# Loading the K and V caches in pairs of tiles: a one-token attention kernel on one core

## The chip, the core and the metric

The kernel runs on one core of one Trainium2 chip. The metric is device time in microseconds (us), the median of several runs, lower is better. The kernel before takes 2529.17 us (three runs, 2528.84 to 2529.18). A profile is one further execution, recorded by the hardware profiler.

In what follows PE is TensorE (matmul), DVE is VectorE, ACT is ScalarE, SP is SyncE, which issues nearly all of the transfers. "L313" is line 313 of the kernel. A core has 16 DMA engines, which work off the transfers that were issued; a transfer spreads over all of them.

## What is computed

One token's attention over a long cache, beside a gated feed-forward, both mixed by a scalar gate. All data are bf16.

```
x: [1, 1, 512]   k_cache, v_cache: [1, 32 heads, 65536 positions, 128]
q = x @ wq                               # 32 heads of 128
scores = (q . k_cache) / sqrt(128)       # per head, 65536 of them
o = softmax(scores) @ v_cache            # per head, 128
a = concat(o) @ wo                       # [4096] @ [4096, 512]
b = (silu(x @ w_gate) * (x @ w_up)) @ w_down
g = sigmoid(sum(x * gate_w))
out = g * a + (1 - g) * b                # [1, 1, 512]
```

The two caches hold 537 MB each, and each number in them is used once. The weights (wq and wo 4 MB each, the feed-forward 5.5 MB) are small beside them.

## The kernel before

**Tiles.** A head's 65,536 positions are cut in four tiles (`G` = 4) of 128 x 128 positions: partition p of a tile holds 128 positions (`NB`) that stand one after the other in memory, each 128 numbers long. So a tile is 4 MB, a contiguous row of 32 KB in each of 128 partitions. There are 128 tiles of K and 128 of V, numbered n = 0 to 127 through all heads (`N`).

**Buffers.** K tiles, V tiles, wq, the feed-forward weights and the second half of wo share a ring of five buffers of 32 KB a partition (`SLOTS`). `take` hands out the buffer that has been free longest, `give` returns it. Nothing is scheduled by a planner: the kernel is written under a manual schedule, so that each engine, SP's queue of transfers included, runs its instructions in the order of the program text. A transfer into a buffer waits on SP until the instructions that read that buffer last are done, and all later transfers wait behind it.

**What happens to a K tile** (`products`, L236; `scores`, L254; `fold`, L268). DVE multiplies the tile by the head's q, which lies spread over all partitions in `q_bc` (L245), and adds the upper half of each 128 products to the lower half, once for the first four tiles, twice for the others (L249). PE sums what is left (64 or 32 columns) by matmuls with an identity matrix, four columns at a time, into a PSUM tile of 128 x 512 (L258: 16 or 8 matmuls). DVE folds the last four columns into the scores (L272).

**What happens when a head's four tiles are scored.** DVE takes the maximum of each partition (L278); ACT, PE and DVE make one maximum of all partitions (L280, L282, L287); ACT takes the exponentials and their sum (L291); PE sums over partitions (L299), and DVE makes the weight of the head (L304, L305). To start this early, the first K tile of the next head is multiplied in two halves of 64 positions, and the steps stand between them.

**What happens to a V tile** (`values`, L307). 32 matmuls of 512 columns (four positions each, L313) add exponentials times V into a PSUM tile of the head. When four tiles are done, `head_turn` (L329) brings the head's result to the partitions (L326, L342, L349), and `project` (L353) multiplies it by its rows of wo (L356) into two accumulators that stay in PSUM to the end. The last eight positions of the last tile are multiplied in another form (L334).

**The order.** wq and the first four K tiles are issued at once. `queries` (L145) makes q for all heads, by matmuls of 512 columns (L147) whose stationary operand is x spread over 128 columns, and ACT copies (L154). Then come the four K tiles of head 0, with the gate and the first half of the feed-forward between them (L176: 112 matmuls of one column). From tile 4 on, a list `steps` (L397) pairs a K tile n with a V tile v. In each step SP issues K tile n (already issued for n = 4) and V tile v, DVE and PE work on K tile n, and PE on V tile v. V starts four tiles behind K; from n = 40 on (`SPREAD`) a step in four carries no V tile until V stands eight tiles behind (`LAG`). The buffers allow some three transfers in flight beside the tiles in use. In the last eight steps only V tiles are left.

**wo.** Its first 16 heads' rows are loaded in four pieces of 512 KB into two small buffers of their own, one for every four heads; the other 16 heads' rows (`LATE`) are issued last of all, behind V, in four pieces, into a ring buffer. The last V tiles are issued in pieces too, ever smaller (`V_CUTS`), so that PE can begin on what has landed.

Of the kernel before, what the change touches and what calls it, by code (L numbers as in the profile page):

```python
# [11 lines left out]
P = 128  # L12
# [3 lines left out]
NB = 128  # L16
SLOTS = 5
# [5 lines left out]
LAG = 8  # L23
SPREAD = 40

WG = 4
LATE = 16
LATE_CUTS = (0, 5, 10, 14, LATE)
TURNED = 8
V_CUTS = {3: (0, 64, NB), 2: (0, 64, NB), 1: (0, 32, 64, 96, 112, NB - TURNED, NB)}  # L30
# [3 lines left out]
def kernel(  # L34
# [26 lines left out]
    QG = 4  # L61
    assert Dh == P and Sk % (NB * P) == 0 and NBH <= 512 and H % QG == 0 and G >= 2
# [5 lines left out]
    ppool = ctx.enter_context(tc.tile_pool(name="ppool", bufs=3))  # L68
    wo_pool = ctx.enter_context(tc.tile_pool(name="wo_pool", bufs=2))
# [11 lines left out]
    def take(name):  # L81
        slot = free.pop(0)
        held[name] = slot
        return ring.tile(
            [P, NB * Dh], bf16, name=name.split(".")[0], tag=f"slot{slot}"
        )
# [5 lines left out]
    consts.tile([P, 32], bf16, name="fill")  # L92
# [6 lines left out]
    QW = QG * Dh  # L99
    wq_t = take("wq_t.0")  # L100
    nc.sync.dma_start(out=wq_t, in_=A_wq.rearrange("(p t) f -> p (t f)", t=KT))
    wq_sb = wq_t.rearrange("p (t f) -> p t f", t=KT)

    K_tiles, V_tiles, S_tiles, F_tiles, P_tiles, O_tiles = {}, {}, {}, {}, {}, {}

    def load(dst, cache, n, name, cuts=(0, NB)):
        h, g = divmod(n, G)
        t = take(f"{name}.{n}")
        view = t.rearrange("p (j d) -> p j d", d=Dh)
        src = cache[0, h, g * NB * P : (g + 1) * NB * P, :].rearrange("(p j) d -> p j d", j=NB)  # L110
        for a, b in zip(cuts[:-1], cuts[1:]):
            nc.sync.dma_start(out=view[:, a:b, :], in_=src[:, a:b, :])
        dst[n] = view

    def load_k(n):
        load(K_tiles, A_k_cache, n, "K_t")

    def load_v(n):
        load(V_tiles, A_v_cache, n, "V_t", V_CUTS.get(N - n, (0, NB)))

    for n in range(G):
        load_k(n)
# [8 lines left out]
    q_bc = consts.tile([P, H * Dh], bf16, name="q_bc")  # L131
    X_bc = consts.tile([P, KT, P], bf16, name="X_bc")
    for t in range(KT):
        nc.vector.tensor_copy(out=X_bc[:, t, :], in_=xT[:, t : t + 1].to_broadcast([P, P]))

    rowsum = consts.tile([P, H], f32, name="rowsum")
# [3 lines left out]
    b_sb = consts.tile([1, D], f32, name="b_sb")  # L140
# [3 lines left out]
    def queries(g):  # L144
        qg_ps = psum_m.tile([P, QW], f32, name="qg_ps", tag="misc")  # L145
        for t in range(KT):
            nc.tensor.matmul(  # L147
                qg_ps,
                lhsT=X_bc[:, t, :],
                rhs=wq_sb[:, t, g * QW : (g + 1) * QW],  # L150
                start=(t == 0),
                stop=(t == KT - 1),
            )
        nc.scalar.activation(out=q_bc[:, g * QW : (g + 1) * QW], in_=qg_ps, func=ACT.Copy)  # L154

    wo_tiles = {}

    def load_wo(g):
        wo_tiles[g] = wo_pool.tile([P, WG, D], bf16, name="wo_sb", tag="wo_sb")
        rows = A_wo[g * WG * P : (g + 1) * WG * P, :]  # L160
        nc.sync.dma_start(out=wo_tiles[g], in_=rows.rearrange("(h p) n -> p h n", p=P))

    def load_late(cuts):
        late = take("wo_late.0")[:, : LATE * D].rearrange("p (h n) -> p h n", n=D)
        rows = A_wo[(H - LATE) * P :, :].rearrange("(h p) n -> p h n", p=P)
        for a, b in zip(cuts[:-1], cuts[1:]):
            nc.sync.dma_start(out=late[:, a:b, :], in_=rows[:, a:b, :])
        return late
# [52 lines left out]
    def feed_forward_out(hT, rest):  # L221
        b_ps = psum_m.tile([1, D], f32, name="b_ps", tag="misc")
        for t in range(FT):
            nc.tensor.matmul(
                b_ps, lhsT=hT[:, t : t + 1], rhs=wd_sb[:, t, :], start=(t == 0), stop=(t == FT - 1)
            )
        nc.scalar.activation(out=b_sb, in_=b_ps, func=ACT.Copy, scale=rest)
        for i, a in enumerate(a_ps):
            nc.tensor.matmul(
                a, lhsT=ones_f[0:1, 0:1], rhs=b_sb[:, i * HD : (i + 1) * HD], start=True, stop=False  # L230
            )
# [4 lines left out]
    def products(n, a=0, b=NB):  # L236
        h = n // G
        K = K_tiles[n][:, a:b, :]
        qb = q_bc[:, h * Dh : (h + 1) * Dh]
        q_rep = bass.AP(  # L240
            tensor=qb.tensor,
            offset=qb.offset,
            ap=[list(qb.ap[0]), [0, b - a], [1, Dh]],
        )
        yield nc.vector.tensor_tensor(out=K, in0=K, in1=q_rep, op=ALU.mult)  # L245
        half = Dh
        while half > width_of(n):
            half //= 2
            yield nc.vector.tensor_tensor(  # L249
                out=K[:, :, 0:half], in0=K[:, :, 0:half], in1=K[:, :, half : 2 * half],  # L250
                op=ALU.add,
            )

    def scores(n):  # L254
# [11 lines left out]
        give(f"K_t.{n}")  # L266
# [18 lines left out]
    def exponentials(h, mT_ps):  # L285
# [4 lines left out]
        P_tiles[h] = ppool.tile([P, NBH], bf16, name="P_sb")  # L290
# [16 lines left out]
    def values(n):  # L307
# [12 lines left out]
        if n < N - 1:  # L320
            del V_tiles[n]
            give(f"V_t.{n}")

    def head_copy(h):
        O_sb = small.tile([4, 4 * Dh], f32, name="O_sb")
        nc.scalar.activation(out=O_sb, in_=O_tiles.pop(h), func=ACT.Copy)  # L326
        return O_sb
# [25 lines left out]
    def project(h):  # L353
        rows = wo_tiles[h // WG][:, h % WG, :] if h < H - LATE else wo_late[:, h - (H - LATE), :]
        for i, a in enumerate(a_ps):
# [3 lines left out]
                rhs=rows[:, i * HD : (i + 1) * HD],  # L359
# [5 lines left out]
    def score_tile(n):  # L365
        for _ in products(n):
            pass
        if n:
            fold(n - 1)

    for g in range(H // QG):
        queries(g)
    give("wq_t.0")
    gu_t = take("gu_t.0")
    wgu_sb = gu_t[:, : 2 * KT * F].rearrange("p (w t f) -> p w t f", w=2, t=KT)
    for w, rows in enumerate((B_w_gate, B_w_up)):
        nc.sync.dma_start(out=wgu_sb[:, w], in_=rows.rearrange("(p t) f -> p t f", t=KT))
    score_tile(0)
    xs = gate_sum()
    scores(0)  # L380
    eg2 = gate_exp(xs)
    wd_t = take("wd_t.0")
    wd_sb = wd_t[:, : FT * D].rearrange("p (t n) -> p t n", t=FT)
    nc.sync.dma_start(out=wd_sb, in_=B_w_down.rearrange("(p t) n -> p t n", t=FT))
    score_tile(1)
    rest = gate_value(eg2)
    scores(1)
    load_k(4)
    score_tile(2)
    scores(2)  # L390
    load_v(0)
    ff = feed_forward_in()
    give("gu_t.0")
    score_tile(3)
    scores(3)

    steps = []  # L397
    v = 0
    for n in range(G, N):
        due = not (n >= SPREAD and n % 4 == 3 and n - v < LAG)  # L400
        steps.append((n, v if due else None))
        v += due
    while v < N:
        steps.append((None, v))
        v += 1

    done = tot_ps = wo_late = None
    for n, v in steps:
        if n is not None and n > G:
            load_k(n)  # L410
        if v is not None:
            if v % (WG * G) == 2 and v // (WG * G) < (H - LATE) // WG:
                load_wo(v // (WG * G))
            if v:
                load_v(v)
            if v == N - 1:
                wo_late = load_late(LATE_CUTS)
        vector = iter(()) if n is None else products(n)
        top_of = None
        if n is None:  # L420
            top_of = H - 1 if F_tiles else None
        elif n % G == 0:
            top_of = n // G - 1
            vector = (i for a in (0, NB // 2) for i in products(n, a, a + NB // 2))
        if top_of is not None:
            next(vector, None)
            fold(top_of * G + G - 1)
            mT_ps = row_max(top_of)
            next(vector, None)
            exponentials(top_of, mT_ps)  # L430
        if n == G:
            hT = feed_forward_mid(*ff)
        for _ in vector:
            pass
        if n is not None and n % G:
            fold(n - 1)
        if tot_ps is not None:
            weight(*tot_ps)
            tot_ps = None
        if n == G:  # L440
            feed_forward_out(hT, rest)
            give("wd_t.0")
        if done is not None:
            head_turn(done, head_copy(done))
        if v is not None:
            values(v)
        if top_of is not None:
            tot_ps = top_of, total(top_of)
        if n is not None:
            scores(n)  # L450
        if done is not None and done < H - LATE:
            project(done)
        done = v // G if v is not None and v % G == G - 1 else None
    head_turn(H - 1, head_copy(H - 1))
    for h in range(H - LATE, H):
        project(h)

    out_sb = consts.tile([1, D], bf16, name="out_sb")
# [33 lines left out]
```

## Time and profile before

| | |
|---|---|
| median of three runs | 2529.17 us |
| the profiled execution | 2529.15 us |
| its span, from its first to its last instruction | 2527.4 us |
| mean granted TensorE clock | 0.772 |
| busy: DVE / PE / ACT | 2083.6 us (82%) / 1523.3 us (60%) / 77.6 us (3%) |
| read from HBM | 1087.64 MB, 430 GB/s over the span |
| chain of work that ended last | DMA 71%, PE 22%, DVE 6% |
| K transfers | 128 of 4096 KB, 36.9 us from issue to landing (median) |
| V transfers | 125 of 4096 KB, 29.2 us, and 10 pieces |
| wo transfers | 4 of 512 KB, 33.8 us, and 4 pieces at the end |

How to read the lines of the profile that follow. A group line names the source line, the engine, the operation, the tile written and the tiles read, their shapes and how often it ran; behind the bar stand its total busy time and the mean of one in ns, and behind the second bar the engine's idle time just before these instructions, with what ended most of it. A timeline line begins with the start and the duration in us; equal instructions that follow each other are merged into one line ("x32"), and square brackets hold the idle time before it and what ended it. Lines of SPq are the issues of transfers; a transfer's work is done by the DMA engines later. The granted clock of TensorE is a share of its full speed; it changes between a half and the whole many times in this span.

### The profile page before, as it was taken

To read this page: it belongs to the slowest core of one execution; us is meant where nothing else is said; L and a number is where in the kernel's file an instruction comes from. 1 tells how busy PE (TensorE), PEld (TensorE's weight loads), DVE (VectorE), ACT (ScalarE), POOL (GpSimd) and SP (SyncE) were. 2 spreads that over 40 slices of the span, in tenths; PEclk is the share of its full clock that TensorE was granted. 3 is DMA by queue.
4 is the path that set the end of the run, shared out by engine and by line. 5 is a ranking of instruction groups with operands and counts; after the bars stand their busy time and mean duration, and the time that the engine had idled before them with its cause. 6 is when DMAs were issued, how large, how long until landed. Compare 5 with 4: busy or idle time off the path is not lost.

```text
span 2527.4 us, 13150 instructions
## 1 busy us (share of the span) xinstructions
PE 1523.3 (60%) x5770; PEld 579.9 (23%) x5770; DVE 2083.6 (82%) x744; ACT 77.6 (3%) x207; POOL 0.7 (0%) x6
## 2 busy tenths in 40 slices
PE   3666556655666555556665666566556665665568
PEld 1322222221222212212222222222222221222223
DVE  6988888788888999988888888888888888888860
ACT  1000000000000000000000000000000000000000
POOL 0000000000000000000000000000000000000000
PEclk7877777777777777787777777777877777777779
DMA  9999999999999999999999999999999999999998
GB/s 415 435 431 431 434 434 432 433 432 431 434 431 435 432 431 433 433 432 434 432 433 432 432 433 434 433 432 432 433 434 433 432 432 432 435 434 432 431 432 370
DMA packets 43019, 1088.49 MB, mean 431 GB/s; under 512 B 4689, under 2 KB 8786, under 8 KB 9170
## 3 DMA queue, kind: packets, MB, share of 16 engines
q1 hardware_dynamic: 42674, 1087.65, 99.9%
q8 instruction: 45, 0.74, 0.1%
q14 instruction: 12, 0.10, 0.0%
q10 hardware_dynamic: 288, 0.00, 0.0%
HBM read 1087.64 MB, written 0.00 MB: 430 GB/s over the span
## 4 chain that ended last, share of the span: by engine, by line
DMA 71%; PE 22%; DVE 6%; issue 0%; ACT 0%; SPq 0%; DVEq 0%
DMA V_t<-in_A_v_cache_dram 65%; PE O_ps L313 21%; DMA K_t<-in_A_k_cache_dram 6%; DVE K_t L245 3%; DVE K_t L249 2%; PE S_ps L258 1%; DMA wo_late<-in_A_wo_dram 0%; DVE S_sb L272 0%; PE oh_ps L342 0%; DVE m L278 0%; ACT P_sb L291 0%; PE a_ps L356 0%; PE mT_ps L282 0%; ACT O_sb L326 0%; DVE top L287 0%
## 5 line engine op out<-in xcount | busy, mean ns | idle before, releaser
L313 PE MATMUL O_ps<-V_t,P_sb 128*4 128x512 bf16 x4094 | 1149.9, 451 | 672.4 <-DMA V_t<-in_A_v_cache_dram 672.4
L245 DVE TENSOR_TENSOR K_t<-K_t,q_bc 128x16384 bf16<-128x16384 bf16 (+1 forms) x159 | 1117.2, 7026 | 346.0 <-DMA K_t<-in_A_k_cache_dram 346.0
L249 DVE TENSOR_TENSOR K_t<-K_t 128x8192 bf16<-128x8192 bf16 (+1 forms) x314 | 859.8, 2738 | 8.6
L313 PEld LDWEIGHTS <-P_sb 128*4 128x4 bf16 x4094 | 392.7, 97 | 1409.4 <-issue 1064.4
L258 PE MATMUL S_ps<-K_t,ident_b 128*128 128x512 bf16 x1056 | 265.3, 395 | 97.3 <-DVE K_t L249 97.1
L258 PEld LDWEIGHTS <-ident_b 128*128 128x128 bf16 x1056 | 98.6, 102 | 245.2 <-issue 156.0
L282 PE MATMUL mT_ps<-diag,ones_f 128*128 128x128 f32 x64 | 23.9, 473 | 141.3 <-ACT diag L280 141.3
L342 PE MATMUL oh_ps<-ident_f,O_sb 4*128 4x1 f32 x256 | 55.5, 334 | 74.5 <-ACT O_sb L326 74.5
L272 DVE TENSOR_REDUCE S_sb<-S_ps 128x128 f32<-128x512 f32 x128 | 87.5, 684 | 4.8 <-PE S_ps L258 4.8
L280 ACT ACTIVATE diag<-ident_f,m 128x128 f32<-128x128 f32 x32 | 12.8, 402 | 2110.1 <-DVE m L278 2110.1
L342 PEld LDWEIGHTS oh_ps<-ident_f,O_sb 4*128 4x128 f32 x256 | 52.8, 301 | 84.1 <-ACT O_sb L326 79.8
L282 PEld LDWEIGHTS mT_ps<-diag,ones_f 128*128 128x128 f32 x64 | 14.9, 289 | 158.4 <-ACT diag L280 158.4
L459 DVE CAST out_sb<-a_ps 1x256 bf16<-1x256 f32 x1 | 0.4, 411 | 58.3 <-PE a_ps L356 58.3
L291 ACT ACTIVATE P_sb<-S_sb,bias 128x512 bf16<-128x512 f32 x32 | 23.1, 722 | 1.0
L278 DVE TENSOR_REDUCE m<-S_sb 128x1 f32<-128x512 f32 x32 | 22.0, 686 | 1.1
L326 ACT ACTIVATE O_sb<-O_ps 4x512 f32<-4x512 f32 x32 | 18.3, 572 | 132.8 <-PE O_ps L313 132.8
L147 PE MATMUL qg_ps<-wq_t,X_bc 128*128 128x512 bf16 x32 | 8.8, 443 | 13.0 <-DMA wq_t<-in_A_wq_dram 13.0
L304 DVE RECIPROCAL recip<-tot_ps 128x1 f32<-128x1 f32 x32 | 5.1, 158 | 12.5 <-PE tot_ps L299 12.5
L299 PEld LDWEIGHTS tot_ps<-rowsum,ones_f 128*128 128x128 f32 x64 | 9.5, 188 | 14.0 <-issue 14.0
L299 PE MATMUL tot_ps<-rowsum,ones_f 128*128 128x1 f32 x64 | 12.2, 260 | 0.0
L349 ACT ACTIVATE oT<-oh_ps,rg 128x1 bf16<-128x1 f32 x32 | 8.4, 264 | 63.4 <-PE oh_ps L342 63.4
L287 DVE TENSOR_REDUCE top<-mT_ps 128x1 f32<-128x128 f32 x32 | 9.1, 284 | 1.0 <-PE mT_ps L282 1.0
(42 smaller groups left out, 68.9 us busy)
## 6 DMA issues: line engine op xcount, KB each, us to landing
K_t<-in_A_k_cache_dram SPq DMA_DIRECT2D x128, 4096.0 KB, 36.9
V_t<-in_A_v_cache_dram SPq DMA_DIRECT2D x125, 4096.0 KB, 29.2
V_t<-in_A_v_cache_dram SPq DMA_DIRECT2D x4, 2048.0 KB, 31.7
wq_t<-in_A_wq_dram SPq DMA_DIRECT2D x1, 4096.0 KB, 12.3
V_t<-in_A_v_cache_dram SPq DMA_DIRECT2D x3, 1024.0 KB, 32.1
wo_sb<-in_A_wo_dram SPq DMA_DIRECT2D x4, 512.0 KB, 33.8
gu_t<-in_B_w_gate_dram SPq DMA_DIRECT2D x1, 1792.0 KB, 34.3
gu_t<-in_B_w_up_dram SPq DMA_DIRECT2D x1, 1792.0 KB, 38.2
```

What stands on the lines that cost most here:

```text
L245: yield nc.vector.tensor_tensor(out=K, in0=K, in1=q_rep, op=ALU.mult)
L249: yield nc.vector.tensor_tensor(out=K[:, :, 0:half], in0=K[:, :, 0:half], in1=K[:, :, half : 2 * half], op=ALU.add,)
L258: nc.tensor.matmul(S, lhsT=ident_b, rhs=K_tiles[n][:, :, c : c + QUAD], start=(c == 0), stop=(c == width - QUAD),)
L272: nc.vector.tensor_reduce(out=S_tiles[h][:, g * NB : (g + 1) * NB], in_=F_tiles.pop(n), axis=AXIS.X, op=ALU.add)
L278: nc.vector.tensor_reduce(out=m, in_=S_tiles[h], axis=AXIS.X, op=ALU.max)
L280: nc.scalar.activation(out=diag, in_=ident_f, func=ACT.Copy, scale=m)
L282: nc.tensor.matmul(mT_ps, lhsT=ones_f, rhs=diag, start=True, stop=True)
L291: nc.scalar.activation(out=P_tiles[h], in_=S_tiles[h], func=ACT.Exp, bias=bias, scale=scale, accum_out=rowsum[:, h : h + 1],)
L299: nc.tensor.matmul(tot_ps, lhsT=ones_f, rhs=rowsum[:, h : h + 1], start=True, stop=True)
L313: nc.tensor.matmul(O_tiles[h], lhsT=P_tiles[h][:, g * NB + j : g * NB + j + 4], rhs=V_tiles[n][:, j : j + 4, :], start=(g == 0 and j == 0) ...
L326: nc.scalar.activation(out=O_sb, in_=O_tiles.pop(h), func=ACT.Copy)
L342: nc.tensor.matmul(oh_ps, lhsT=O_sb[:, c * Dh : (c + 1) * Dh], rhs=ident_f[0:4, c : c + 1], start=(c == 0 and not turned), stop=(c == 3),)
```

## The change

- The ring has three buffers of 64 KB a partition in place of five of 32 KB. K and V tiles are loaded in pairs: a transfer is 8 MB, with a contiguous row of 64 KB in each partition. The first and the last pair of K, and the last three of V, are still loaded in pieces.
- What DVE and PE do is still done tile by tile, each on its half of the pair. A buffer is given back when both halves are used.
- `queries` makes q with the weights as the stationary operand, by 128 matmuls of one column, into one column per head. A head's q is spread over the partitions shortly before it is needed (`query`): ACT scales an identity matrix by q, PE multiplies it by ones, ACT copies the result.
- The feed-forward's three weights share one buffer, the one that wq held. The first half of wo is loaded into a ring buffer behind the last pair of K, and all of the first 16 heads are projected together in the last pass over K; the second half is loaded behind V, as before.
- The main loop runs over pairs of K tiles, i = 0 to 63. V stands two pairs behind: pass i multiplies V pair i - 2. The first K tile of a head is no longer multiplied in halves.

```diff
-SLOTS = 5
+PAIR = 2 * NB
+SLOTS = 3
...
+LAST = (0, 64, 128, 160, 192, 224, 240, PAIR - TURNED, PAIR)
+V_CUTS = {3: (0, NB, PAIR), 2: (0, NB, PAIR), 1: LAST}
+EARLY = 16
+LATE_CUTS = (EARLY, 21, 26, 30, 32)
...
+    def load(dst, cache, m, name, cuts=(0, PAIR)):
+        h, g = divmod(m, MH)
+        view = take(f"{name}.{m}").rearrange("p (j d) -> p j d", d=Dh)
+        rows = cache[0, h, g * PAIR * P : (g + 1) * PAIR * P, :]
+        src = rows.rearrange("(p j) d -> p j d", j=PAIR)
         for a, b in zip(cuts[:-1], cuts[1:]):
             nc.sync.dma_start(out=view[:, a:b, :], in_=src[:, a:b, :])
-        dst[n] = view
+        for i in range(2):
+            dst[2 * m + i] = view[:, i * NB : (i + 1) * NB, :]
...
+    def load_k(m):
+        load(K_tiles, A_k_cache, m, "K_t", (0, NB, PAIR) if m in (0, M - 1) else (0, PAIR))
...
+    load_k(0)
+    load_k(1)
...
+    def queries():
+        q_ps = psum_m.tile([P, H], f32, name="q_ps", tag="misc")
+        for h in range(H):
+            for t in range(KT):
+                nc.tensor.matmul(
+                    q_ps[:, h : h + 1],
+                    lhsT=wq_sb[:, t, h * Dh : (h + 1) * Dh],
+                    rhs=xT[:, t : t + 1],
+                    start=(t == 0),
+                    stop=(t == KT - 1),
+                )
+        nc.scalar.activation(out=qT, in_=q_ps, func=ACT.Copy)
+
+    def query(h):
+        diag = small.tile([P, P], bf16, name="q_diag")
+        nc.scalar.activation(out=diag, in_=ident_f, func=ACT.Copy, scale=qT[:, h : h + 1])
+        qb_ps = psum_m.tile([P, P], f32, name="qb_ps", tag="misc")
+        nc.tensor.matmul(qb_ps, lhsT=ones_b, rhs=diag, start=True, stop=True)
+        q_tiles[h] = small.tile([P, P], bf16, name="q_sb")
+        nc.scalar.activation(out=q_tiles[h], in_=qb_ps, func=ACT.Copy)
...
-        give(f"K_t.{n}")
+        if n % 2:
+            give(f"K_t.{n // 2}")
...
+    mT_ps = tot_ps = None
+    for i in range(M):
+        h, first = i // MH, i % MH == 0
+        vector = products(2 * i)
+        next(vector)
+        if mT_ps is not None:
+            exponentials(h - 1, mT_ps)
+        if not first:
+            fold(2 * i - 1)
         for _ in vector:
             pass
+        if i == M - 1:
+            for o in range(EARLY):
+                project(o)
+            give("wo_early.0")
+            load_v(M - 2)
+        scores(2 * i)
+        if i == 0:
+            xs = gate_sum()
+            eg2 = gate_exp(xs)
+        if i >= 2:
+            values(2 * i - 4)
+            values(2 * i - 3)
+            if i < M - 2:
+                load_v(i - 1)
+        if mT_ps is not None:
+            tot_ps = total(h - 1)
+            mT_ps = None
+        if first and i > MH:
+            head_turn(h - 2, head_copy(h - 2))
+        vector = products(2 * i + 1)
+        next(vector)
+        fold(2 * i)
+        if i == 1:
+            hT = feed_forward_mid(*ff)
+            feed_forward_out(hT, rest)
+            give("guw_t.0")
+            load_v(0)
+        for _ in vector:
+            pass
...
+        if not first and h + 1 < H:
+            query(h + 1)
+        scores(2 * i + 1)
+        if i == 0:
+            ff = feed_forward_in()
+        if i + 2 < M:
+            load_k(i + 2)
+        elif i + 2 == M:
+            wo_sb = load_wo("wo_early.0", (0, EARLY))
+            load_v(M - 3)
+        if not first:
+            fold(2 * i + 1)
+            mT_ps = row_max(h)
+    load_v(M - 1)
+    exponentials(H - 1, mT_ps)
+    tot_ps = total(H - 1)
+    head_turn(H - 2, head_copy(H - 2))
+    values(N - 4)
+    values(N - 3)
+    weight(H - 1, tot_ps)
+    wo_sb = load_wo("wo_late.0", LATE_CUTS)
+    values(N - 2)
+    values(N - 1)
     head_turn(H - 1, head_copy(H - 1))
-    for h in range(H - LATE, H):
+    for h in range(EARLY, H):
         project(h)
```

## The prediction

> **What bounds the kernel now.** I read the span by slices first, then the DMA queues, then the waits, then the timeline of one steady stretch. The slices say that the DMA engines never rest:
>
> ```profile
> DMA  9999999999999999999999999999999999999998
> GB/s 415 435 431 431 434 434 432 433 432 431 434 431 435 432 431 433 433 432 434 432 433 432 432 433 434 433 432 432 433 434 433 432 432 432 435 434 432 431 432 370
> ...
> q1 hardware_dynamic: 42674, 1087.65, 99.9%
> ```
>
> Packets of the one large queue fill 99.9% of 16 engines' span. So time goes only if the same 1,087.65 MB move with less overhead, and time comes with every microsecond in which the queue runs dry. The groups show the compute engines waiting for these transfers, with room left:
>
> ```profile
> L313 PE MATMUL O_ps<-V_t,P_sb 128*4 128x512 bf16 x4094 | 1149.9, 451 | 672.4 <-DMA V_t<-in_A_v_cache_dram 672.4
> L245 DVE TENSOR_TENSOR K_t<-K_t,q_bc 128x16384 bf16<-128x16384 bf16 (+1 forms) x159 | 1117.2, 7026 | 346.0 <-DMA K_t<-in_A_k_cache_dram 346.0
> ```
>
> The steady timeline gives the pace and the depth of the queue:
>
> ```profile
> 1236.14 9.91 PE L313 MATMUL O_ps<-V_t,P_sb 128*4 128x512 bf16 x32 [6.70 <-DMA V_t<-in_A_v_cache_dram]
> ...
> 1245.74 8.69 DVE L245 TENSOR_TENSOR K_t<-K_t,q_bc 128x16384 bf16<-128x16384 bf16 x1 [2.96 <-DMA K_t<-in_A_k_cache_dram]
> ...
> 1246.08 0.33 SPq L112 DMA_DIRECT2D V_t<-in_A_v_cache_dram  x1
> 1247.91 0.33 SPq L112 DMA_DIRECT2D K_t<-in_A_k_cache_dram  x1
> 1254.47 6.75 DVE L249 TENSOR_TENSOR K_t<-K_t 128x8192 bf16<-128x8192 bf16 x2
> 1255.45 8.80 PE L313 MATMUL O_ps<-V_t,P_sb 128*4 128x512 bf16 x32 [7.57 <-DMA V_t<-in_A_v_cache_dram]
> 1264.18 1.91 PE L258 MATMUL S_ps<-K_t,ident_b 128*128 128x512 bf16 x8
> ```
>
> A V tile and a K tile arrive every 19.3 us (1236.14 to 1255.45), 9.65 each. The V transfer issued at 1246.08 is used at 1274.85 (the next L313 burst of the timeline): 28.8 us from issue to use for 9.65 us of transfer, so some 19 us of work always stand queued. That reserve is what the change spends.
>
> The profiled execution took 2529.15 us: span 2527.4 and 1.75 around it. The median of the runs is 2529.17, so the sum stands against it as it is. A change under 0.2% (5.1 us) can't be told from none.
>
> **1. Packets, a gain.** A contiguous row is one packet today: by the trace's packet records a 32 KB row takes 1213 ns, 16 KB 611, 1 KB 46. The slope is 36.75 ps a byte, so 9 ns of a packet are fixed. Packets overlap a little: on the engine that is ahead, a tile's eight packets and the semaphore's pass in 9.680 us (median), of which 8 x 1.204 = 9.634 is bytes: 46 ns of overhead a tile. Some 123 of the 128 pairs go as one transfer of 64 KB rows. If a row stays one packet, a pair loses one tile's overhead: 123 x 46 ns = **-5.6 us**. Bounds: -1.1 if rows are cut at 32 KB (one 9 ns semaphore record a pair), -10 if all nine fixed 9 ns go. I take -5.5; "row = packet" holds for every size shown.
>
> **2. The queries, nothing.** L147's 32 matmuls (8.78 us from 13.04) become 128 of one column; the same form at L176 ran 112 in 6.83 us, 61 ns each, so 7.8 us. Then come q's copy (0.2), diag (0.40, row L280), a matmul (0.3) and a copy (0.31, L127): q is ready at about 22.3, K's first half at 22.8 (DVE's start today). The 31 later spreads are two ACT instructions and one matmul a head, on an ACT that is busy 3%, ahead of scores that have 15 us to spare (3). If q were late, the first K tile would start that much later; bounds 0 to 2, inside the range of 4. DVE loses its half-tile forms (about 14 us in all); it waits for K anyway.
>
> **3. The steady loop, no gap, with little in hand.** The ring falls into two buffers for K and one for V: V's next pair is issued only when the last has been used up. Clock this from the moment at which V pair a has left the engines. They go on with a K pair for 19.3 us, then need V pair a+1. V lands at 0.3 (last packet to semaphore, from the end of the trace). Scores of the tile ahead: K landed at -19.0, DVE takes 8.69 + 6.75 + 0.68, so PE starts them at -2.9, and eight cold matmuls (the granted clock is half at the head of a burst: 0.427 us apart there, 0.216 later) end at 0.5. Then 64 value matmuls at 0.2175 (96 in 20.88 us in the tail) are 13.9. Cold stretches at the head of bursts last 2.1 to 5.5 us, of which scores take 3.4, so values pay up to 1.1 more. The SP issue costs 0.1, and from issue to flow it takes 1.9 (first load: issue 0.74, first packet 1.83, and that packet 0.8 longer than 1213 ns). Sum 16.4 to 17.5 against 19.3: **1.8 to 2.9 us in hand**, where today there are 19. The K buffer comes free after scores of the pair's second half, at about 19, and is needed at 36. I take 0; bounds 0 to +61 for each microsecond by which the loop overruns (61 pairs).
>
> Behind it one smaller cost: the 16 engines drift apart. The first and last of a load's 16 semaphore increments are 0.3 us apart at the start, 8.7 at the end, in steps of about 1.3. A queue of 19 us let the others run ahead; one of 2 us does not. **+1.5** (0 to 6).
>
> **4. The start, a gap.** Up to the first two K pairs nothing changes. Then V pair 1 must wait until V pair 0 is used. DVE: pair 0 from 22.8 to 50.4 (as today), pair 1 from its landing at 51.8: 8.69 + 0.68 + 4.43, then 8.68 + 0.68 + 0.8 (L213 to L218), to 75.8. L224 (4.9) frees the feed-forward buffer at 80.8, before K pair 2 ends at 83.6 (the feed-forward weights land at 64.6 as today, less 0.3, plus 19.3): no gap for V pair 0, which flows to 103, and K pair 3 to 122.4. DVE's second half ends at 80.2, scores run behind L229 to 87 to 89, fold and max to about 90; the next tile's 15.7 gives 105.8, scores 2 to 3.4, values 14 to 15: V pair 1 is issued at 122 to 125 and flows 1.9 later. **+3** (0 to 6).
>
> **5. The tail, PE becomes the bound.** Today:
>
> ```profile
> 2466.05 20.88 PE L313 MATMUL O_ps<-V_t,P_sb 128*4 128x512 bf16 x96
> ...
> 2516.08 3.18 PE L313 MATMUL O_ps<-V_t,P_sb 128*4 128x512 bf16 x14 [0.26 <-DMA V_t<-in_A_v_cache_dram]
> 2519.19 0.35 PE L334 MATMUL oh_ps<-P_sb,V_t 128*128 128x1 bf16 x8
> ...
> 2520.98 3.87 PE L356 MATMUL a_ps<-wo_late,oT 128*1 128x256 bf16 x32
> ```
>
> PE keeps up with V's last pieces, and wo's last piece lands at 2523.95, 3.45 before the end. Afterwards the last scores stand on PE behind the values of V's third-last pair, whose second half lands at T. Then: values 7.0, scores 1.9, fold, max, diag, mT, top, bias and exponentials 0.68 + 0.69 + 0.40 + 0.5 + 0.28 + 0.2 + 0.91 and some 0.5 between, total and head turn 0.4 + 1.9: T + 15.4. Four tiles are 27.4, half cold at first +1.9: T + 44.7. From the last L313 to the end today is 8.1: T + 52.8. By DMA alone: two pairs 38.6, wo's half 5.4, and 3.45: T + 47.5. The difference is 5.3; I take **+5** (2 to 7), since a warm PE would spare 1.9.
>
> wo's first half is one 2 MB load of the same 1 KB rows as four loads today, issued ahead of its turn: 0.
>
> **Sum:** 2529.15 - 5.5 + 1.5 + 3 + 5 = 2533.2, so **2533**. Its own range is 2526 to 2541.
>
> **Rivals.**
> A. One V buffer gates the DMA (slower). Decides from 19.3 us: if landing, values and restart of part 3 take longer, each pair waits by the excess: 1 us gives 2533 + 61 = 2594. For it: a cold PE, and a restart measured only on an idle queue. Against it: the rows leave 1.8. Chance 0.15. The Trainium skill, "Trainium Kernel Development and Optimization", Best Practices, says "Double-buffer for performance: Overlap DMA with compute", and V is no longer double-buffered; no run here shows yet what that costs.
> B. Rows are cut at 32 KB: 2533 + 4.4 = 2538. No row above 32 KB is shown. Chance 0.10.
> C. The doubled distance between rows slows the reads: 1% of 2499 us (1087.65 MB at 36.75 ps a byte over 16 engines) is 25 us: 2558. Against it: 14 KB, 16 KB and 32 KB packets share one slope. Chance 0.04. The Trainium skill, "DMA: Bandwidth & Descriptors", Latency and other measured facts, has copies losing speed as the distance between rows grows over powers of two, first seen at 512 KiB, which is eight times what stands here; no run shows it.
> D. Faster: the tail stays with the DMA (warm PE, 2), the start's gap closes (0), drift costs 0, packets give 8: 2523. Chance 0.14.
> The forecast has 0.57.
>
> **Chances.** Faster: D and 0.03 of the forecast's own, 0.17. Same (2524.1 to 2534.2): 0.40, two thirds of the forecast and a little of B. Slower: 0.43: the rest. Range: below 2521 almost nothing; above 2548 lie most of A and C, 0.18.
>
> **What would show it.** Part 1: packets of 64 KB at about 2418 ns, some 16,000 fewer in the queue's line. Part 3: DVE's K waits and PE's V waits keep a 38.6 us rhythm, DMA share stays at 9s. Part 4: one dip between 80 and 130 us. Part 5: L313 without waits over its last 120 matmuls, and the end some 8 us after the last landing. Wrong would be a rhythm over 38.7 us, or 32 KB packets.

## The result and the profile after

The changed kernel takes 2541.82 us (median of four runs, 2538.82 to 2544.16) against 2529.02 (four, 2528.84 to 2529.18): ratio 1.005, 95% interval 1.0038 to 1.0061, so 12.8 us slower. The forecast was 2533 us, in a range of 2521 to 2548.

The profiled execution is the shortest of the four, 2538.82 us, with a span of 2537.0: 9.6 us over the span before. What is read from this trace explains these 9.6. That other executions take up to 5 us more, while the four before lie within 0.4 us, is a finding of its own.

The page of the changed kernel, slices and large queue:

```profile
DMA  9999999999999999999999999999999999999998
GB/s 414 422 429 422 431 422 435 434 431 431 430 432 433 430 433 435 428 430 433 432 433 432 435 434 430 432 434 432 430 434 435 431 429 434 430 433 431 435 422 360
...
q1 hardware_dynamic: 24770, 1087.65, 99.5%
```

The same bytes go in 24,770 packets in place of 42,674. But where the row of GB/s was level at 431 to 435, it now dips to 422 in the second, fourth and sixth slice, and the share of the queue is 99.5% where it was 99.9%. By stages of the span (start and end, length, busy time of PE, its weight loads, DVE, ACT and POOL with the numbers of instructions, granted clock, DMA share, GB/s):

```profile
0.00:270.00 270.00, 131.31 (x696) 54.69 (x697) 210.93 (x71) 10.90 (x30) 0.70 (x6) 0.77 0.99 421
270.00:1000.00 730.00, 383.80 (x1619) 150.53 (x1618) 605.24 (x188) 25.05 (x74) 0.00 (x0) 0.75 1.00 432
```

Before, these stages ran at 429 and 433:

```profile
0.00:270.00 270.00, 156.07 (x651) 62.77 (x652) 220.04 (x86) 13.36 (x30) 0.70 (x6) 0.78 1.00 429
270.00:1000.00 730.00, 427.11 (x1574) 159.63 (x1573) 630.51 (x222) 21.06 (x58) 0.00 (x0) 0.76 1.00 433
```

So in this execution most is lost in the first 270 us, and a little all along. Counted in bytes (the moment at which the engines together had moved so much, a packet under way counted by its share), the changed kernel is 2.1 us behind at 55 MB, 5.8 at 200, 7.3 at 900 and 8.3 at 1085. By finished packets alone, which are twice as long after the change, some 0.5 to 1.2 us more come out on the way, which comes near the 6.5 us at 200 MB that an expectation below names.

The start, in the timeline of the changed kernel, value matmuls and V's issues alone:

```profile
107.51 13.97 PE L312 MATMUL O_ps<-V_t,P_sb 128*4 128x512 bf16 x64
121.51 0.33 SPq L111 DMA_DIRECT2D V_t<-in_A_v_cache_dram  x1
...
145.88 15.19 PE L312 MATMUL O_ps<-V_t,P_sb 128*4 128x512 bf16 x64
161.11 0.33 SPq L111 DMA_DIRECT2D V_t<-in_A_v_cache_dram  x1
...
185.84 15.69 PE L312 MATMUL O_ps<-V_t,P_sb 128*4 128x512 bf16 x64 [1.43 <-DMA V_t<-in_A_v_cache_dram]
201.56 0.33 SPq L111 DMA_DIRECT2D V_t<-in_A_v_cache_dram  x1
...
225.74 16.21 PE L312 MATMUL O_ps<-V_t,P_sb 128*4 128x512 bf16 x64 [1.05 <-DMA V_t<-in_A_v_cache_dram]
```

Each V pair is issued as soon as the last of the 64 matmuls that use the pair before it is done: 107.51 + 13.97 = 121.48, issue at 121.51. The passes are 38.4, 40.0 and 39.9 us apart (from 107.51 on), where two pairs take 38.6 on the engines. And the same 64 matmuls take longer each time. The windows around the first and the fourth burst show that the clock differs:

```profile
107.50:121.50 14.00, 14.00 (x66) 5.45 (x65) 12.30 (x4) 0.00 (x0) 0.00 (x0) 1.00 1.03 441
225.70:242.00 16.30, 16.26 (x66) 5.91 (x66) 11.19 (x4) 0.00 (x0) 0.00 (x0) 0.86 0.94 407
```

PE is busy throughout both; the granted clock is 1.00 in the first and 0.86 in the fourth. A late V pair is only part of the reason. In this trace the clock changes between a half and the whole on one fixed grid of 3.41 us, and each of its 67 rises comes at the end of a step in which PE stood idle for 0.8 us at most. PE starts each pass with scores, and how much of the values behind them still runs at half clock depends on where in the grid the scores begin: the second burst had no wait in front of it and took 15.19 us, 2.5 of them at half clock. In front of the third and the fourth burst the wait for V (1.43 and 1.05 us) fell into the step at whose end the clock would have risen, so that it rose a step later. The fifth (at 265.44 us) waited 1.07 us just after the rise and took 13.97. Over the 60 bursts of whole pairs in the stream, the nine with a wait of over 0.3 us in front take 14.5 us in the mean and the others 14.4.

In the middle of the span the rhythm holds, with little room:

```profile
1251.46 0.33 SPq L111 DMA_DIRECT2D V_t<-in_A_v_cache_dram  x1
...
1256.78 8.69 DVE L243 TENSOR_TENSOR K_t<-K_t,q_sb 128x16384 bf16<-128x16384 bf16 x1 [2.01 <-DMA K_t<-in_A_k_cache_dram]
...
1291.08 0.33 SPq L111 DMA_DIRECT2D V_t<-in_A_v_cache_dram  x1
...
1295.30 8.69 DVE L243 TENSOR_TENSOR K_t<-K_t,q_sb 128x16384 bf16<-128x16384 bf16 x1 [3.54 <-DMA K_t<-in_A_k_cache_dram]
```

K pairs land 38.5 us apart here. (From the first to the last full burst of values, 60 passes, the mean is 38.9.) DVE starts as soon as a K pair has landed, that is, about 0.3 us after the slowest engine has finished it. So V was issued 5.0 us and 3.9 us ahead of that moment: these few microseconds are the whole reserve, where it was 19.

The end:

```profile
2485.06 7.07 PE L312 MATMUL O_ps<-V_t,P_sb 128*4 128x512 bf16 x32 [2.58 <-DMA V_t<-in_A_v_cache_dram]
2492.06 1.90 PE L256 MATMUL S_ps<-K_t,ident_b 128*128 128x512 bf16 x8
...
2500.15 29.03 PE L312 MATMUL O_ps<-V_t,P_sb 128*4 128x512 bf16 x126
...
2530.90 3.65 PE L353 MATMUL a_ps<-wo_late,oT 128*1 128x256 bf16 x32
```

The last 126 value matmuls run without a wait. The last piece of wo lands at 2530.40, 6.45 us later than before, and the span ends 6.6 us behind it, where it was 3.45: 9.6 us = 6.45 of the stream and 3.15 of the tail.

The packet records close the account of the 9.6 us. Up to the last landing of wo, an engine stands without a packet for 9.1 us in the mean of the 16, where it was 7.0. Its packets take 12.3 us longer than the usual time of their size, where it was 2.5. The end behind the last landing grew by 3.2. What is left of the span, the usual time of the packets, fell from 2514.4 to 2509.0 us. So 2.1 + 9.8 + 3.2 - 5.4 = 9.7: most of the loss isn't idle time but longer packets. Why a packet takes longer when a transfer is issued late stays open; of the longer time at V's issues, 84% falls on the first packet that each engine moves.

### The profile page after: what moved, and what is told of

It is laid out like the page before. It is cut to its first block, busy times and chain, and to the rows that moved or that the text cites. A ratio compares the mean times of both kernels' runs of the same rounds, so it can differ in the third digit from the quotient of the medians.

```text
span 2537.0 us, 13082 instructions
## 1 busy us (share of the span) xinstructions
PE 1359.2 (54%) x5898; PEld 538.3 (21%) x5898; DVE 2066.1 (81%) x648; ACT 90.8 (4%) x264; POOL 0.7 (0%) x6
## 3 DMA queue, kind: packets, MB, share of 16 engines
q1 hardware_dynamic: 24770, 1087.65, 99.5%
## 4 chain that ended last, share of the span: by engine, by line
DMA 53%; PE 28%; DVE 18%; issue 0%; ACT 0%; SPq 0%; another core or an unknown queue 0%; DVEq 0%; ACTq 0%
DMA K_t<-in_A_k_cache_dram 44%; PE O_ps L312 21%; DVE K_t L243 10%; DMA V_t<-in_A_v_cache_dram 10%; DVE K_t L247 7%; PE S_ps L256 6%; DVE S_sb L271 1%; PE b_ps L224 0%; PE qb_ps L159 0%; PE oh_ps L340 0%; PE a_ps L353 0%; SPq L111 0%; PE tot_ps L298 0%; PE a_ps L230 0%
## 5 line engine op out<-in xcount | busy, mean ns | idle before, releaser
L243 DVE TENSOR_TENSOR K_t<-K_t,q_sb 128x16384 bf16<-128x16384 bf16 x128 | 1112.1, 8688 | 204.2 <-DMA K_t<-in_A_k_cache_dram 204.2
L312 PE MATMUL O_ps<-V_t,P_sb 128*4 128x512 bf16 x4094 | 923.2, 387 | 13.2 <-DMA V_t<-in_A_v_cache_dram 11.6
L256 PE MATMUL S_ps<-K_t,ident_b 128*128 128x512 bf16 x1056 | 355.4, 495 | 1070.7 <-DVE K_t L247 1070.7
L247 DVE TENSOR_TENSOR K_t<-K_t 128x8192 bf16<-128x8192 bf16 x252 | 849.3, 3370 | 4.3
L312 PEld LDWEIGHTS <-P_sb 128*4 128x4 bf16 x4094 | 350.9, 86 | 604.6 <-issue 105.0
L256 PEld LDWEIGHTS <-ident_b 128*128 128x128 bf16 x1056 | 117.9, 115 | 1248.6 <-issue 1100.8
L161 ACT ACTIVATE q_sb<-qb_ps 128x128 bf16<-128x128 f32 x32 | 8.9, 277 | 1148.6 <-PE qb_ps L159 1148.6
L281 PE MATMUL mT_ps<-diag,ones_f 128*128 128x128 f32 x64 | 16.3, 338 | 62.0 <-ACT diag L279 62.0
L340 PE MATMUL oh_ps<-ident_f,O_sb 4*128 4x1 f32 x256 | 34.3, 251 | 0.5 <-ACT O_sb L324 0.5
L340 PEld LDWEIGHTS oh_ps<-ident_f,O_sb 4*128 4x128 f32 x256 | 31.6, 190 | 1.0 <-ACT O_sb L324 0.5
L279 ACT ACTIVATE diag<-ident_f,m 128x128 f32<-128x128 f32 x32 | 12.8, 401 | 129.9 <-DVE m L277 129.9
```

Source lines behind the costliest of these rows:

```text
L247: yield nc.vector.tensor_tensor(out=K[:, :, 0:half], in0=K[:, :, 0:half], in1=K[:, :, half : 2 * half], op=ALU.add,)
L256: nc.tensor.matmul(S, lhsT=ident_b, rhs=K_tiles[n][:, :, c : c + QUAD], start=(c == 0), stop=(c == width - QUAD),)
L279: nc.scalar.activation(out=diag, in_=ident_f, func=ACT.Copy, scale=m)
L281: nc.tensor.matmul(mT_ps, lhsT=ones_f, rhs=diag, start=True, stop=True)
L312: nc.tensor.matmul(O_tiles[h], lhsT=P_tiles[h][:, g * NB + j : g * NB + j + 4], rhs=V_tiles[n][:, j : j + 4, :], start=(g == 0 and j == 0) ...
L340: nc.tensor.matmul(oh_ps, lhsT=O_sb[:, c * Dh : (c + 1) * Dh], rhs=ident_f[0:4, c : c + 1], start=(c == 0 and not turned), stop=(c == 3),)
```

## The experiments

Two theories stood against each other. **Late issue:** 64 KB packets bring what was forecast, and V's issue, though inside the 19.3 us, comes too close to the moment at which the engines run out. **Packets:** the 64 KB rows or the doubled distance between them are slow in themselves. Later runs ask how much lead is needed, what the tail costs, and how far the packets carry alone. "After" is the changed kernel; its median is 2541.82. Each edit is against it, unless said otherwise.

**e1_rows32: a pair is still one transfer, but of two rows of 32 KB a partition**

```diff
-        src = rows.rearrange("(p j) d -> p j d", j=PAIR)
+        src = rows.rearrange("(t p j) d -> p t j d", t=2, j=NB)
...
+            if b - a == PAIR:
+                nc.sync.dma_start(out=view.rearrange("p (t j) d -> p t j d", t=2), in_=src)
```

> Each pair still comes as one 8 MB transfer into the same three buffers, in the same order, but with two rows of 32 KB in a partition (each pair holds two tiles as the kernel before cuts them). Packet theory of the prediction: 64 KB packets save 46 ns a pair, so this loses some 4.5 us: about 2546 us. Rival, that rows of 64 KB or their distance are slow in themselves (64 KB packets average 2430 ns, 12 above their usual 2418): this gains 5 us or more, 2537 or less. Both agree that the order of V and K issues stays as it is.

Measured: 2548.98 (2546.68 to 2553.52), ratio 1.0081 (1.0067 to 1.0094), 7.2 above after. The theory of slow packets falls: with the rows of before, the kernel loses more. No run here shows the loss over distance that the page "DMA: Bandwidth & Descriptors" of the Trainium skill (Latency and other measured facts) puts at far larger distances: with half the distance the time rose.

**e2_less16: 16 of the 64 value matmuls of nearly every V pair left out, so that V is issued earlier**

```diff
-        for j in range(0, end, 4):
+        js = list(range(0, end, 4))
+        if n % 2 and n < N - 8:
+            js = js[16:]
+        for j in js:
```

> Leaves out the first 16 of the 64 value matmuls of every V pair but the last four pairs, so that a V buffer comes free 3.5 us earlier; transfers and everything else stay. Late-issue theory: V is issued 4.7 us (2.8 to 5.9) before the slowest engine runs dry and the queue needs about 4 to go on without loss; with 8 in hand the loss of the first 270 us (6 to 7 us against the kernel before) goes: 2534 to 2536 us, the tail unchanged. Rival, packet size: no change, 2541.

Measured: 2530.47 (2527.27 to 2532.36), ratio 1.0003 (0.9994 to 1.0012). It fell 11.3 us, further than the 6 to 8 expected. Nothing was changed but the number of value matmuls (half of one V tile's sum is missing in each pair), and with it the moment at which V's buffer comes free. So late issue costs about 11 us here, unless fewer matmuls help by themselves; the table below, which holds kernels with 64, 72 and 80 matmuls a pair beside each other, speaks against that. In the profiled execution, the slowest of the ten, the last piece of wo lands 10.6 us earlier than in after and 4.1 earlier than before the change, but the span ends 10.7 us behind that landing in place of 6.6, since PE ran longer at half clock there (the 32 value matmuls before the last scores took 10.02 us in place of 7.07, the 126 behind them 29.84 in place of 29.03).

**e3_more8 and e4_more16: 8 or 16 value matmuls of each such pair done twice, V issued 1.74 or 3.48 us later**

```diff
+        if n % 2 and n < N - 8:
+            js = js[:-1] + js[-9:-1] + js[-1:]     # e4: js[-17:-1]
```

> Repeats 8 value matmuls of every V pair but the last four pairs (their products are added twice), so that a V buffer comes free 1.7 us later: 3.0 us in hand in place of 4.7. If a restart needs 1.9 us, as the prediction took from the first load of the run, nothing is lost: 2541 to 2544 us. If it needs about 4 us in the stream, every pair loses about 1 us: 2580 to 2610.

> As e3_more8, with 16 value matmuls repeated: V comes free 3.5 us later than in the changed kernel. If V's release gates the queue, the loss grows one for one with the delay: e3 lost 0.92 us a pair at 1.74, so this loses 2.66 on 60 pairs, 160 us: about 2700 us. If e3's loss came from something else (PE busier, the clock), it grows less: 2600 to 2660.

Measured: e3 2597.28 (2590.39 to 2614.09), ratio 1.0279 (1.0249 to 1.031); e4 2668.54 (2657.11 and 2679.96), ratio 1.0551 (1.0506 to 1.0597). The page of e3:

```profile
q1 hardware_dynamic: 24770, 1087.65, 98.5%
...
L315 PE MATMUL O_ps<-V_t,P_sb 128*4 128x512 bf16 x4574 | 1033.9, 388 | 37.9 <-DMA V_t<-in_A_v_cache_dram 37.2
```

1.74 us later cost 55.5 us over 60 pairs, 0.92 us each; 3.48 later cost 126.7 (two runs), 2.1 each, between the two figures expected of e4. With 1.8 us to spare, e3 would have cost next to nothing. So the reserve of the forecast is not there. But it isn't a threshold at 3.9 us either, as e4's expectation had it from e3 alone (3.0 us of lead and the 0.92 that were lost): a threshold would give e4 1.74 us a pair more than e3, and it gives 1.2.

**The loss against the lead.** This settles it, from the packet records of seven kernels (after, e1 to e5, e8; 59 V issues each). For each V issue, the lead is the time from SP's issue to the moment at which the fastest of the 16 engines ends the K pair before it (a load's semaphore, the counter that tells of its landing, goes up once for each engine; the first of these 16 increments, less 0.3 us, is that moment). The loss is the time that the engines then stood without a packet, plus what V's packets took over their usual 2418 ns (1213 for 32 KB), each as a mean of 16 engines. 354 of the 413 issues fall into these rows; the others lie beyond them on either side:

```
lead of the fastest engine, us   issues   loss, us   idle   longer packets
-1.0 to -0.5                        11      2.22     1.56       0.66
-0.5 to  0.0                        14      1.74     1.00       0.74
 0.0 to  0.5                        22      1.35     0.66       0.69
 0.5 to  1.0                        37      1.01     0.40       0.61
 1.0 to  1.5                        29      0.73     0.28       0.46
 1.5 to  2.0                        49      0.31     0.07       0.25
 2.0 to  2.5                        74      0.19     0.04       0.14
 2.5 to  3.0                        67      0.08     0.03       0.06
 3.0 to  3.5                        51      0.04     0.02       0.02
```

Roughly one curve serves all seven, though they differ in their number of matmuls: between 0.5 and 1.0 us of lead, each kernel that has such issues loses 0.7 to 1.2 us in the mean. It has no edge: the loss fades until the fastest engine has 2.5 to 3 us of work left, which for the slowest, some 2.3 us behind it, is about 5. In after, the medians are 2.4 and 4.7. Added up over the 59 issues, the loss is 2.9 us in e2, 8.7 in e8, 12.9 in after, 63.1 in e3 and 144.8 in e4: against after -10.0, -4.2, +50.2 and +131.9, where the medians of the runs moved by -11.3, -4.4, +55.5 and +126.7, and the last landing of wo, in the very executions that were traced, by -10.6, -6.6, +50.4 and +136.8.

**e8_less16_start: the edit of e2 for the first eight V pairs alone**

```diff
+        if n % 2 and n < 16:
+            js = js[16:]
```

> The changed kernel with 16 of 64 value matmuls left out for V pairs 0 to 7 alone (the first 400 us). If the loss is made in the first passes, as the bytes moved by 200 MB say (6.5 us behind the kernel before, then level), most of e2's 11 us come back: 2533 to 2536 us. If it is spread over all pairs: 2540.

Measured: 2537.47 (2533.25 to 2542.69), ratio 1.0034 (1.0021 to 1.0047): 4.4 us of e2's 11.3. Neither expectation is met: the first eight issues of V pairs 1 to 8 lose 5.2 us in after and 0.4 here, the 51 others 7.7 in after, about 0.15 each. So in these two traces the start is some 40% of the loss, and the rest is spread thin. The medians alone don't settle it: the six runs of e8 reach from under the four of after to within 1.5 us of their slowest.

A third trace says that the loss need not fall at the start. e5 below is the changed kernel itself up to its last four V tiles. Its V pairs 0 to 8 lose 2.3 us in place of 6.8, its first 270 us run at 428 GB/s in place of 421, and its other 51 issues lose 13 in place of 7.7, with the deepest dip in the slices 24 and 25 of its page:

```profile
GB/s 414 435 431 430 430 430 438 433 432 434 432 430 430 431 431 427 427 434 428 430 432 432 434 424 417 429 429 431 430 432 431 431 436 437 432 432 431 431 428 383
```

How much is lost is set by the short lead; where it falls differs from execution to execution.

**e5_tail_half: every second value matmul of the last four V tiles left out**

```diff
-        for j in range(0, end, 4):
+        for j in range(0, end, 4 if n < N - 4 else 8):
```

> Leaves out every second value matmul of the last four V tiles, some 13.5 us of PE work behind the last softmax. If PE is the bound of the tail, the end falls back to the last landing of wo: the span ends some 4 us after it in place of 6.6, about 2539 us. If the transfers bound the tail: no change, 2541 to 2542.

Measured: 2535.49 (2531.83 to 2545.45), ratio 1.003 (1.0018 to 1.0042), 6.3 under after where about 3 were expected. In its timeline PE waits for V again near the end, as it did before the change:

```profile
2523.17 1.02 PE L312 MATMUL O_ps<-V_t,P_sb 128*4 128x512 bf16 x4 [1.42 <-DMA V_t<-in_A_v_cache_dram]
...
2527.39 5.40 PE L353 MATMUL a_ps<-wo_late,oT 128*1 128x256 bf16 x32 [0.20 <-DMA wo_late<-in_A_wo_dram]
```

The span ends 4.3 us after the last landing (2531.03), 2.3 less than in after. That PE binds the tail is shown. What that is worth is only bracketed, 2.3 us in the traces and 6.3 by the medians, since executions of this kernel differ by 13.6 us.

**e6_vtiles: K in pairs with two buffers, V in single tiles with two buffers of its own**

```diff
-SLOTS = 3
+K_SLOTS = 2
+V_SLOTS = 2
...
             values(2 * i - 4)
+            if i < M - 1:
+                load_v(2 * i - 2)
+            else:
+                load_v(N - 3)
             values(2 * i - 3)
-            if i < M - 2:
-                load_v(i - 1)
+            if i < M - 1:
+                load_v(2 * i - 1)
```

V's tiles have 32 KB buffers here, and one is always loading while the other is used. The first half of wo and one V tile share a K buffer at the end, and the first 16 heads are projected while PE would wait for the last exponentials.

> K stays in pairs of 64 KB rows (two buffers), V goes back to tiles of 32 KB with two buffers of its own, so a V tile is issued 10 us before the queue ends; near the end a K buffer takes wo's first half and V tiles, wo's first half comes behind two V tiles, and its projections stand in the wait for the last softmax. Late-issue theory: the start's loss (some 7 us) and the tail's (3 to 4) go, half of the packets' gain (2.8) is lost: 2527 to 2530 us, as the kernel before or 2 us under it. Rival, packet size: half of the loss stays, about 2535.

Measured: 2527.2 (2526.57 to 2528.29, eleven runs), ratio 0.9993 (0.9984 to 1.0002). The rate by stages of e6:

```profile
0.00:270.00 270.00, 134.09 (x726) 56.69 (x727) 216.01 (x72) 10.90 (x30) 0.70 (x6) 0.79 1.00 431
270.00:1000.00 730.00, 385.05 (x1605) 149.00 (x1604) 607.02 (x188) 25.05 (x74) 0.00 (x0) 0.75 1.00 433
```

The rate of the first stage is 431 against 421 in after, and the time is 14.6 us under after with 64 KB packets kept for K. (Of the 11.7 us between the two traced executions, 9.2 are the stream, by the last landing of wo, and the rest is the end, which e6 rearranges too.) That agrees with the rule of the Trainium skill ("Trainium Kernel Development and Optimization", Best Practices) that the prediction quoted: V double-buffered is level with the kernel before, V in one buffer is 0.5% slower. It is the best version here. Its eleven runs all lie below the 21 runs of the kernel before beside them (2528.83 to 2529.56), but by the interval 1.9 us isn't told from none.

**e7_vtiles_rows32: e6 with rows of 32 KB**

```diff
-        src = rows.rearrange("(p j) d -> p j d", j=PAIR)
+        src = rows.rearrange("(t p j) d -> p t j d", t=2, j=NB)
```

(against e6; K pairs are still one transfer, and V's tiles are cut to match)

> e6_vtiles with 32 KB rows for K too, still one transfer a pair: a deep queue and no 64 KB packets. The packets' gain by itself is 61 pairs x 46 ns = 2.8 us: 2530.0 us against e6's 2527.2. If 64 KB packets gain nothing, 2527.

Measured: 2529.6 (2529.04 to 2531.1, eleven runs), ratio 1.0002 (0.9993 to 1.0012). Beside e6 this prices the packets alone, in a loop that doesn't lose: 2.4 us for 61 K pairs, 39 ns a pair where the forecast had 45.

## Why the prediction was right or wrong

The time rose, as the forecast's terms said, but by +12.8 us at the median against +4. The side was barely forecast: slower had a chance of 0.43, same 0.40. 2541.82 lies inside 2521 to 2548 but just outside the forecast's own range of 2526 to 2541; what lies above that range was kept for rivals A to C, and it is a mild form of A's mechanism that came. So the hit owes something to luck: packets, queries and tail were forecast well, the loop was not. The profiled execution, step by step:

- **Part 1, packets (-5.5): right.** A 64 KB row stays one packet, of 2418 ns as extrapolated, 15,744 of them. e7 against e6 gives 39 ns a pair, which over 123 pairs is 4.8 us. The packet records give as much: without idle time, longer packets and the end, the spans of the three kernels with 32 KB rows (before, e1, e7) are 2513.5 to 2514.4 us, those of the six with 64 KB rows 2508.7 to 2509.5, and e6, with 64 KB for K alone, 2511.5. Before against after is 5.4, 44 ns a pair.
- **Part 2, queries (0): right.** K's first half was what DVE waited for; at 30 MB the streams are less than 0.1 us apart. The 128 matmuls took 3.57 us where 7.8 were forecast. DVE started at 24.34, not at 22.8: the last of the 16 engines brought its part of that half 1.5 us later than before.
- **Part 3, the loop (0) with drift (+1.5): mis-sized; this is the step that failed.** When V is issued was forecast well: 1.8 to 2.9 us in hand behind a restart of 1.9 means a lead of 3.7 to 4.8, and the median is 4.7 to the slowest engine. What was wrong is what that lead must cover. The 1.9 us, from a first load on an idle queue, are right for an engine that has run out: at the latest issues of e3 and e4 1.8 to 1.9 us are lost behind the issue. But a lead of 1.9 doesn't buy the loss off: it was counted to the slowest engine, and the fastest runs out 2.3 us earlier; and with 2 us left to the fastest, 0.2 are still lost, most of it in longer first packets. "1.8 to 2.9 us in hand" was in truth nothing in hand. The forecast's own sign of being wrong, a rhythm over 38.7 us, came: the mean is 38.9. Drift and restart were two separate terms in the forecast; they are one. Over the pairs behind the start it comes to 7.7 us in place of 1.5 (13 in e5).
- **Part 4, the start (+3): the dip came in this execution, but longer; in e5 there is hardly one.** V pair 1 was issued at 121.5 (forecast 122 to 125). V pair 0 lost 1.6 us that the forecast had at nothing, and pairs 1 to 8 lost 5.2: 6.8 in all. The forecast closed the account with pair 1. In fact the bursts that follow it run partly at half clock and grow from 13.97 to 16.21 us, two of them because PE had waited for a late V pair, and the next pair is late as well. Part 3 had allowed the values 1.1 us for a clock still at half; here it was up to 2.3. In e5 V pairs 0 to 8 lose 2.3 us, near the +3.
- **Part 5, the tail (+5): right in its place.** From the landing of the second half of V's third-last pair (2485.02) to the end are 52.0 us, forecast 52.8; the last matmuls don't wait. The tail adds 3.15 us to the profiled span and not 5, as the stream ended later too: the last landing came 45.4 us behind that point, where the forecast had 44.0. The end is 6.6 us behind the last landing, forecast some 8.

The sum with the measured terms is -5.4 + 7.7 + 6.8 + 3.15 = +12.3 against the 9.6 us of the profiled spans. The 2.7 us between them are losses that the kernel before has as well: the packet records hold 9.6 us of idle time and longer packets before and 21.4 after, so that the change adds 11.9 and not 14.5. Parts 3 and 4 together had 4.5.

**The rivals.** A has the right mechanism, one V buffer gating the DMA, but the wrong point: it was to decide from 19.3 us, by the whole excess. By an estimate from the curve it decides from some 16.2 us, counted as A counts, with the restart of 1.9 in it (19.3 less the 5 us of lead that the slowest engine needs, plus 1.9), and gently at first; the forecast's own sum was 16.4 to 17.5. e3 shows how steep it gets: 1.74 us more and it is 68 us over the kernel before. B (rows cut at 32 KB) and C (slow reads) are refuted by the packet records (64 KB packets at 2418 ns), C by e1 as well: with 32 KB rows the longer packets cost 15.8 us, not less than the 12.3 of after. D hoped for a closed start and a warm PE; neither came.

**Still open** is why executions of after differ by 5.3 us. The spread stays in e2 (5.1), where V is early, in e5 (13.6), e8 (9.4) and e3 (23.7); it falls to 1.7 and 2.1 in e6 and e7. So it goes with the single V buffer rather than with the mean lead. The traces of after and e5, the same program up to the last tiles, show the losses at different places; what starts them there isn't known, and only one execution of each kernel has a trace.

## What to carry to other kernels

Larger transfers save a fixed few tens of nanoseconds each, and that is easily worked out; the buffer that is given up for them costs nothing only while the next transfer is issued well before the queue runs dry. Count that lead to the DMA engine that runs out first, take it from the slowest burst of the compute engine and not from one at full clock, and ask for clearly more than the restart seen on an idle queue. If it is short, split the buffer whose refill is on the critical path (V, in e6) and keep the large transfers for the one that has time.

## What the runs showed of the hardware

- A transfer issued as the engines run out loses about 1.2 us of idle time and 0.65 us in longer first packets (e3, e4); the longer packets remain, fading, until the fastest engine has some 2.5 us of work left, when the idle time has gone.
- A deep queue lets the 16 engines drift apart (the increments of one load lie 0.3 us apart at the start and 8.7 at the end of the kernel before); with a queue of a few microseconds they stay some 2.2 us apart (median of after; eight in ten loads 1.8 to 3.0).
- The packet's usual time is linear up to 64 KB: 611 ns for 16 KB, 1213 for 32 KB, 2418 for 64 KB.
- In the trace of after the granted clock changes on one grid of 3.41 us, and all 67 rises end a step in which PE stood idle for 0.8 us at most. So the same 64 matmuls last 13.97 us at 1.00 or up to 16.21 at 0.86, depending on where in the grid PE began; a wait of 1.0 to 1.4 us for V cost two bursts a further step, and a third, just behind a rise, nothing.
